# A decode-attention kernel whose second result row is gathered to one partition: two column pieces of 256 and 320, two copies, one run of 1152 bytes

## Chip, cores, metric

One core of one Trainium2 chip. The metric is the device time of one execution in microseconds (us), median over the runs named. Each kernel's time is set beside runs of the kernel before on the same chip in the same rounds. All runs count as fast or, single ones, as unknown; no slow state appeared. Ratios are the mean time of one kernel's fast runs over that of the other's of the same rounds, so they are not quite the ratios of the medians that I quote.

The names in the traces: PE is TensorE, which multiplies matrices (PEld its weight loads); DVE is VectorE, ACT ScalarE, and SP the SyncE, which issues the transfers (DMA). SBUF is the on-chip memory for data, PSUM the one that takes PE's sums; both have 128 partitions, and four groups of 32 of them are called quadrants here. A transfer has landed when the last increment of its semaphore is recorded. The granted clock is the share of TensorE's full clock that the trace records. Of a store, a "run" is a piece of adjacent bytes; elsewhere a run is one execution.

## The reference

Two problems A and B of the same shape: one token, 32 query heads, 16 key/value heads, head size 128, model width 576. A attends to the last 2048 positions of its cache, B to all 8192.

```python
q = (x @ wq).reshape(B, Sq, Hq, Dh)            # 576 -> 32 heads x 128
scores = einsum("bhqd,bhkd->bhqk", q, k) * Dh ** -0.5
o = einsum("bhqk,bhkd->bhqd", softmax(scores), v)
out = o.reshape(B, Sq, Hq * Dh) @ wo           # 4096 -> 576
# result: concat([A's out, B's out]), shape (1, 1, 1152), bf16
```

## The kernel before

Only the end matters: the last product with `wo`, the copy of the sums out of PSUM, and the store. The 4096 rows of `wo` are taken as 32 "rows" jj of 128 partitions each; each row's 576 columns are cut in pieces, and piece j accumulates in partition 32·j of one PSUM bank. Only partition 32·j of each quadrant holds a result.

```python
OUTS = [2, 4]                                  # A in 2 pieces of 288 columns, B in 4 of 144

def wo_part(P, lo, n, off, res):               # rows lo .. lo+n of problem P
    def mm(pe):
        for jj in range(lo, lo + n):
            w = DM // OUTS[P]
            for j in range(OUTS[P]):
                o = off + (jj - lo) * DM + j * w
                ins = pe.matmul(ktps[P][32 * j:32 * j + 32, 0:w], lhsT=opj[:, P, jj:jj + 32],
                                rhs=slots[:, o:o + w], start=(jj == 0), stop=(jj == HQ - 1))
        return ins
    add("pe", mm, reads=[("opj", P)] + res, writes=[("bank", P)])

def finish_out(P):
    n = OUTS[P]
    add("dve", lambda dve: dve.tensor_copy(outsb[0:32 * n, P, 0:DM // n], ktps[P][0:32 * n, 0:DM // n]),
        reads=[("bank", P)], writes=[("outsb", P)])
    # ... then SP stores n runs, one from each partition 32*j
# ...
wo_loads = [(0, 0, 32, ...),                   # A, all 32 rows in one load
            (1, 0, 21, ...), (1, 21, 7, ...), (1, 28, 3, ...), (1, 31, 1, ...)]   # B in four loads
for P, lo, n, off, res in wo_loads:
    load_wo(P, lo, n, off, res)
combine([NG - 1])                              # last group's heads, waits for DVE
o_columns(1)
for P in range(2):
    ...                                        # wo_part of each load of P, then
    finish_out(P)
```

The program orders its own instructions: `add` names what each reads and writes, and semaphore waits follow. One rule of it plays a part:

```python
for r in op.reads:
    w = self.writer.get(r)
    if w is not None:
        deps.append((w, True))
    if r[0] == "bank":                         # PSUM: a reader also waits for earlier readers
        deps += [(o, False) for o in self.readers.get(r, ())]
```

Of the kernel before, what the change touches and what calls it, by code (L numbers as in the profile page):

```python
# [4 lines left out]
BF16 = mybir.dt.bfloat16  # L5
F32 = mybir.dt.float32
ALU = mybir.AluOpType
ACT = mybir.ActivationFunctionType
# [5 lines left out]
DM = 576  # L14
# [4 lines left out]
NG = 5  # L19
NKT = 4  # L20
WQ_W = 18432
OUTS = [2, 4]


class Op:
# [11 lines left out]
class Program:  # L37
# [15 lines left out]
    def add(self, eng, fn, reads=(), writes=(), dma=None, after=(), tag=None, inc=1, loop=None):  # L53
        op = Op(eng, fn, tuple(reads), tuple(writes), dma, tag, inc if dma is None or inc > 1 else 16, loop)
        deps = []
# [4 lines that stand above are left out]
            if r[0] == "bank":  # L60
                deps += [(o, False) for o in self.readers.get(r, ())]
        for r in after:
            deps += [(o, False) for o in self.readers.get(r, ())]
        for r in op.writes:
            w = self.writer.get(r)
            if w is not None:
                deps.append((w, False))
            deps += [(o, False) for o in self.readers.get(r, ())]
        for r in op.reads:
            self.readers.setdefault(r, []).append(op)  # L70
        for r in op.writes:
            self.writer[r] = op
            self.readers[r] = []
        for o, raw in deps:
            if o is op:
                continue
            if o.dma is None and o.eng == eng and (not raw or eng in ("pe", "sp")):
                continue
            op.deps.append(o)
            o.needed = True  # L80
        op.order = len(self.ops)
        self.ops.append(op)
        return op
# [192 lines left out]
def bass_concat_heads__sliding_block_cached__gqa_block_cached__decode_kernel(  # L276
# [31 lines left out]
    add = prog.add  # L308
# [28 lines left out]
    acc = nc.alloc_sbuf_tensor("acc", [128, NG, DH], F32)  # L337
    accs = nc.alloc_sbuf_tensor("accs", [128, NG, DH], F32)
    opj = nc.alloc_sbuf_tensor("opj", [128, 2, 64], BF16)
    outsb = nc.alloc_sbuf_tensor("outsb", [128, 2, DM // 2], BF16)  # L340
    warm = nc.alloc_sbuf_tensor("warm", [128, 8], F32)

    ktps = [nc.alloc_psum_tensor("ktps%d" % b, [128, 512], F32) for b in range(4)]
# [73 lines left out]
    def load_v(g):  # L417
# [19 lines left out]
        reads=["ident"], writes=["twice"])  # L437
    add("pe", lambda pe: pe.matmul(misc[:, 320:338], lhsT=twice[:, :], rhs=xnine[:, :, :].rearrange("p a r -> p (a r)"),  # L438
                                   start=True, stop=True),
        reads=[("xnine", 0), ("xnine", 1), "twice"], writes=[B_M])  # L440
# [243 lines left out]
    def wo_part(P, lo, n, off, res):  # L684
        def mm(pe):
            for jj in range(lo, lo + n):
                w = DM // OUTS[P]
                for j in range(OUTS[P]):
                    o = off + (jj - lo) * DM + j * w
                    ins = pe.matmul(ktps[P][32 * j:32 * j + 32, 0:w], lhsT=opj[:, P, jj:jj + 32],  # L690
                                    rhs=slots[:, o:o + w], start=(jj == 0), stop=(jj == HQ - 1))
            return ins
        add("pe", mm, reads=[("opj", P)] + res, writes=[("bank", P)])


    def finish_out(P):
        n = OUTS[P]
        add("dve", lambda dve: dve.tensor_copy(outsb[0:32 * n, P, 0:DM // n], ktps[P][0:32 * n, 0:DM // n]),  # L698
            reads=[("bank", P)], writes=[("outsb", P)])

        def put(eng):
            src = bass.AP(tensor=outsb, offset=P * DM // 2, ap=[[32 * DM, n], [1, DM // n]])
            dst = out[0, 0:1, P * DM:(P + 1) * DM].rearrange("o (j n) -> (o j) n", j=n)
            return eng.dma_start(dst, src)
        add("sp", put, reads=[("outsb", P)], writes=[("out", P)], dma="out%d" % P)


    WQ = [(4 * SLOT - WQ_W, [("v", 2)]), (SLOT, [("k", 1, 0), ("k", 1, 1), ("v", 0)])]
    for P in range(2):
        off, res = WQ[P]  # L710
# [10 lines left out]
        reads=["kindA"], writes=["sameA"])  # L721
# [3 lines left out]
        reads=["sameB0"], writes=["sameB"])  # L725
# [3 lines left out]
    def pick_A(dve):  # L729
# [8 lines left out]
        reads=["sameB0", "pickB"], writes=["pickB"])  # L738
# [3 lines left out]
        reads=["four"], writes=["maskP"])  # L742
# [35 lines left out]
    for P in range(2):  # L778
        for Q, lo, n, off, res in wo_loads:
            if Q == P:  # L780
                wo_part(P, lo, n, off, res)
        finish_out(P)
    prog.emit()
    for P in range(2):
        o = prog.writer[("out", P)]
# [28 lines left out]
```

## Time and profile before

| | |
|---|---|
| time, median | 245.98 us (245.89 to 246.21, 3 runs) |
| span in the profile | 244.6 us |
| share of the load queue, 16 DMA engines | 98.1% |
| B's last weights land | 242.24 us |
| PE's last matmul ends | 242.54 us |
| store issued / last increment of its semaphore | 242.92 / 244.54 us |

Times inside a run are counted from the span's start. A line of the timeline gives start, duration, engine, source line, operation, tiles, count, and in brackets how long the engine was idle before and what ended that. Where I give a third decimal, it is from the trace's single records of instructions, DMA packets and semaphore increments. The lines themselves stand in the prediction below.

### The profile page before, as it was taken

The page shows a single profiled execution, that of the slowest core. Times are in us where ns is not written, and L with a number is a line of the kernel's source. Part 1 is how long each engine was busy: PE and PEld are TensorE (multiplying, and loading weights), DVE is VectorE, ACT ScalarE, POOL GpSimd, SP SyncE. Part 2 cuts the span into 40 slices and gives each one's busy share as a digit, 9 for nine tenths or more (in the row PEclk, how much of TensorE's full clock was granted, in tenths as well). Part 3 has the DMA queues.
Part 4 walks back from the last instruction along what each step waited for, and adds up shares of the span by engine and source line. Part 5 has one row for each costly group of instructions (what it writes and reads, how often), then busy time and mean ns, then how long its engine had stood idle before and what let it go on. Part 6 is the DMA issues. An engine that isn't in the chain of part 4 may idle for free. (4 is left out here: it accounts for less than half of the span.)

```text
span 244.6 us, 5211 instructions
## 1 busy us (share of the span) xinstructions
PE 165.4 (68%) x2325; PEld 121.3 (50%) x2325; DVE 88.2 (36%) x152; ACT 92.7 (38%) x95; POOL 6.3 (3%) x33
## 2 busy tenths in 40 slices
PE   0007339968389995393999362999457799945965
PEld 0002139746236773233887221987232787624854
DVE  0001407864316454203556302455322246543031
ACT  2000016855306686102678300687600378630000
POOL 5000100000000000000000000000000000000000
PEclk9999957997759999569899859799957589975599
DMA  9999999999999999899999999999989999989993
GB/s 338 434 410 418 434 437 426 429 426 426 445 426 430 482 407 450 380 439 429 478 439 429 413 418 429 434 504 397 461 375 434 429 488 397 461 388 428 414 409 135
DMA packets 4068, 102.88 MB, mean 421 GB/s; under 512 B 602, under 2 KB 732, under 8 KB 988
## 3 DMA queue, kind: packets, MB, share of 16 engines
q1 hardware_dynamic: 3900, 102.76, 98.1%
q8 instruction: 6, 0.10, 0.2%
q10 hardware_dynamic: 160, 0.00, 0.0%
q14 instruction: 2, 0.02, 0.0%
HBM read 102.76 MB, written 0.00 MB: 420 GB/s over the span
## 5 line engine op out<-in xcount | busy, mean ns | idle before, releaser
L506 ACT ACTIVATE kt<-ktps 128x1024 bf16<-128x1024 bf16 x80 | 79.5, 1036 | 89.6 <-PE ktps L496 89.6
L496 PE MATMUL ktps<-ident,slots 128*128 128x128 bf16 x1280 | 87.8, 234 | 22.5 <-PEq L214 19.2
L496 PEld LDWEIGHTS ktps<-ident,slots 128*128 128x128 bf16 x1280 | 81.7, 106 | 38.0 <-issue 37.9
L509 DVE COPY kt<-ktps 128x1024 bf16<-128x1024 bf16 x80 | 60.7, 768 | 59.0 <-PE ktps L496 59.0
L588 PE MATMUL opsum<-slots,ptm 128*32 128x512 bf16 x320 | 28.5, 532 | 9.8 <-PEq L214 9.8
L521 PE MATMUL sacc<-kt,qst 128*32 128x512 bf16 x320 | 25.4, 392 | 2.2 <-PEq L214 2.2
L588 PEld LDWEIGHTS opsum<-slots,ptm 128*32 128x32 bf16 x320 | 14.0, 129 | 22.9 <-issue 20.6
L559 PE MATMUL misc<-ident,psb 128*128 128x128 bf16 x40 | 4.6, 285 | 15.8 <-PEq L214 15.8
L547 ACT ACTIVATE psb<-sacc,stat 128x2048 bf16<-128x2048 f32 x5 | 9.8, 1967 | 10.1 <-DVE stat L536 10.1
L606 DVE TENSOR_TENSOR vtmp<-opsum,maskV 128x512 f32<-128x512 f32 x4 | 2.8, 692 | 30.2 <-PE opsum L588 30.2
L559 PEld LDWEIGHTS misc<-ident,psb 128*128 128x128 bf16 x40 | 3.4, 125 | 18.2 <-issue 18.2
L438 PE MATMUL misc<-xnine,twice 64*128 64x18 bf16 x1 | 0.2, 170 | 18.0 <-DMA xnine<-in_B_x_dram 18.0
L566 DVE TENSOR_TENSOR ptm<-misc,maskP 128x1024 bf16<-128x1024 bf16 x5 | 3.5, 691 | 16.0 <-PE misc L559 16.0
L521 PEld LDWEIGHTS sacc<-kt,qst 128*32 128x32 bf16 x320 | 5.0, 94 | 8.3 <-issue 4.6
L438 PEld LDWEIGHTS misc<-xnine,twice 64*128 64x128 bf16 x1 | 0.1, 99 | 18.0 <-issue 18.0
L462 ACT ACTIVATE qrow<-opsum 128x512 bf16<-128x512 f32 x1 | 0.6, 597 | 19.4 <-PE opsum L456 19.4
L690 PE MATMUL ktps<-slots,opj 128*32 128x144 bf16 (+1 forms) x192 | 6.7, 247 | 0.7 <-issue 0.5
L690 PEld LDWEIGHTS ktps<-slots,opj 128*32 128x32 bf16 x192 | 5.3, 96 | 1.9 <-issue 0.6
L447 DVE TENSOR_SCALAR xpad<-misc,par 128x5 bf16<-128x5 f32 (+1 forms) x8 | 1.2, 229 | 13.8 <-PE misc L438 13.8
L481 POOL COPY qst<-qcol 128x32 bf16<-128x32 bf16 x8 | 1.7, 211 | 147.4 <-PE sacc L521 147.4
L559 PE MATMUL turned<-ident,psb 128*128 128x128 bf16 x40 | 5.3, 313 | 0.0
L534 DVE TENSOR_REDUCE stat<-sacc 128x1 f32<-128x512 f32 x5 | 3.5, 691 | 4.4 <-PE sacc L521 4.4
(75 smaller groups left out, 52.9 us busy)
## 6 DMA issues: line engine op xcount, KB each, us to landing
slots<-in_B_k_cache_dram SPq DMA_DIRECT2D x8, 4096.0 KB
slots<-in_A_k_cache_dram SPq DMA_DIRECT2D x4, 2048.0 KB
slots<-in_A_v_cache_dram SPq DMA_DIRECT2D x4, 2048.0 KB
slots<-in_A_wq_dram SPq DMA_DIRECT2D x1, 4608.0 KB, 13.8
slots<-in_B_wq_dram SPq DMA_DIRECT2D x1, 4608.0 KB, 24.0
slots<-in_A_wo_dram SPq DMA_DIRECT2D x1, 4608.0 KB, 18.7
slots<-in_B_wo_dram SPq DMA_DIRECT2D x1, 3024.0 KB, 25.5
slots<-in_B_wo_dram SPq DMA_DIRECT2D x1, 1008.0 KB, 7.7
```

The source lines that it names most:

```text
L481: return pool.tensor_copy(dst, src)
L496: ins = pe.matmul(ktps_bf[q][:, t * 128:(t + 1) * 128], lhsT=slots[:, o:o + 128], rhs=ident[:, :], start=True, stop=True, is_transpose=True)
L506: add("act", lambda act, src=src, dst=dst: act.activation(dst, src, ACT.Copy), reads=[("bank", q)], writes=[("kt", u % NKT, q)], tag="e%d% ...
L509: add("dve", lambda dve, src=src, dst=dst: dve.tensor_copy(dst, src), reads=[("bank", q)], writes=[("kt", u % NKT, q)], tag="e%d%d" % (u, q))
L521: ins = pe.matmul(sacc[32 * j:32 * j + 32, :], lhsT=qst[:, o:o + 32], rhs=rhs, start=(u == 0 and e == 0), stop=True, skip_group_check=True)
L534: add("dve", lambda dve: dve.tensor_reduce(st(C_M + g), sacc[:, :], AX.X, ALU.max), reads=[B_S], writes=[("st", C_M + g)], tag="max")
L547: return act.activation(dst, src, ACT.Exp, bias=st(C_NB + g), scale=SCALE, accum_out=st(C_L + g))
L559: ins = pe.matmul(dst[:, t * 128:(t + 1) * 128], lhsT=psb[:, o:o + 128], rhs=ident[:, :], start=True, stop=True, is_transpose=True)
L566: return dve.tensor_tensor(ptm[:, c * 1024:(c + 1) * 1024].rearrange("p (t y) -> p t y", t=8), dst.rearrange("p (t y) -> p t y", t=8), mas ...
L588: ins = pe.matmul(opsum[64 * j + 32 * x:64 * j + 32 * x + 32, :], lhsT=ptm[:, o:o + 32], rhs=v[:, at[0], at[1], :, :, b:b + 128], start=(n ...
L606: add("dve", lambda dve: dve.tensor_tensor(vtmp[:, :, :], src, by, ALU.mult), reads=[B_O, w], writes=["vtmp"], tag="keep")
L690: ins = pe.matmul(ktps[P][32 * j:32 * j + 32, 0:w], lhsT=opj[:, P, jj:jj + 32], rhs=slots[:, o:o + w], start=(jj == 0), stop=(jj == HQ - 1))
```

## The change

The intent: a store of one run instead of four needs all of B's result in one partition. Two pieces instead of four, one for DVE and one for ACT, keep the copies at one for each engine, and the widths 256 and 320 balance the two engines. A stays as it was.

```diff
-OUTS = [2, 4]
+PIECES = [[288, 288], [256, 320]]
...
-                w = DM // OUTS[P]
-                for j in range(OUTS[P]):
-                    o = off + (jj - lo) * DM + j * w
+                for j, w in enumerate(PIECES[P]):
+                    o = off + (jj - lo) * DM + sum(PIECES[P][:j])
...
+    def finish_B():
+        lo = 0
+        for j, (name, w) in enumerate(zip(("dve", "act"), PIECES[1])):
+            def go(eng, j=j, lo=lo, w=w):
+                dst, src = outsb[0:1, DM + lo:DM + lo + w], ktps[1][32 * j:32 * j + 1, 0:w]
+                return eng.activation(dst, src, ACT.Copy) if j == 1 else eng.tensor_copy(dst, src)
+            add(name, go, reads=[("bank", 1)], writes=[("outsb", 1, j)]).key = ("out", "piece")
+            lo += w
+        add("sp", lambda sp: sp.dma_start(out[0, 0:1, DM:2 * DM], outsb[0:1, DM:2 * DM]),
+            reads=[("outsb", 1, j) for j in range(2)], writes=[("out", 1)], dma="out1")
```

## The prediction

> **What bounds the kernel now**
>
> I read the page's share of DMA and its queues first, then the chain that ended last, then the instructions of the last ten microseconds one by one.
>
> The page of the kernel before:
>
> ```profile
> q1 hardware_dynamic: 3900, 102.76, 98.1%
> HBM read 102.76 MB, written 0.00 MB: 420 GB/s over the span
> ```
>
> The SP load queue keeps the 16 DMA engines busy for 98% of the span. For some 240 us the kernel is a stream of loads, and this change touches no load. It touches only what follows the last bytes, so the question is what the tail is worth. The chain in order of time, window 233 to 246 us:
>
> ```profile
> 233.52 8.35 DMA slots<-in_B_wo_dram
> 241.87 0.04 issue
> 241.92 0.65 PE ktps L690 x16
> 242.56 0.02 issue
> 242.59 0.31 DVE outsb L698
> ```
>
> Columns: start, duration, what. The last of B's output weights land at 241.87 and 242.24; 16 matmuls, one DVE copy, and the store of the result follow. The timeline of the same tail shows how PE came there:
>
> ```profile
> 235.74 4.79 PE L690 MATMUL ktps<-slots,opj 128*32 128x288 bf16 x136
> 239.25 0.45 DVE L698 CAST outsb<-ktps 64x288 bf16<-64x288 f32 x1 [3.62 <-PE ktps L690]
> 239.73 3.77 SPq L704 DMA_DIRECT2D out_dram<-outsb  x2
> 240.98 0.68 PE L690 MATMUL ktps<-slots,opj 128*32 128x144 bf16 x30 [0.46 <-issue]
> 241.92 0.62 PE L690 MATMUL ktps<-slots,opj 128*32 128x144 bf16 x16 [0.26 <-DMA slots<-in_B_wo_dram]
> 242.59 0.31 DVE L698 CAST outsb<-ktps 128x144 bf16<-128x144 f32 x1 [2.89 <-PE ktps L690]
> ```
>
> Brackets: idle time before, and what ended it. PE does 64 matmuls of A (32 rows in 2 pieces), then 128 of B (32 rows in 4 pieces). It has slack in B: it idles 0.46 and 0.26 us waiting for weights. So the end hangs on loads now, but with PE only about 1.3 us behind (the gaps below). This is the number that decides.
>
> By groups, window 228 to 246 us (last columns: busy us, mean ns; idle):
>
> ```profile
> L690 PE MATMUL ktps<-slots,opj 128*32 128x288 bf16 x64 | 4.1, 286 | 0.0
> L690 PE MATMUL ktps<-slots,opj 128*32 128x144 bf16 x128 | 3.1, 228 | 0.7 <-issue 0.5 <-DMA slots<-in_B_wo_dram 0.3
> L698 DVE CAST outsb<-ktps 64x288 bf16<-64x288 f32 x1 | 0.5, 450 | 3.6 <-PE ktps L690 3.6
> L698 DVE CAST outsb<-ktps 128x144 bf16<-128x144 f32 x1 | 0.3, 307 | 2.9 <-PE ktps L690 2.9
> ```
>
> B has twice A's matmuls and takes less PE time: in B four matmuls stream side by side, in A two. The single records of the trace give the pitch. In A a pair starts at 235.368, 235.490, 235.613 ... 238.920: 122.5 ns per row. In B a set of four starts every 62.5 ns (239.105, 239.168, 239.230). Both are columns/2.4 ns + 2.5 ns: 288/2.4 = 120, 144/2.4 = 60. A row costs the time of its widest piece, not the sum of its pieces.
>
> **What the Trainium skill says**
>
> - "TensorE: Matmul & The Clock Gate", Part 3 (packing small matmuls): matmuls on different column tiles run concurrently and start about 4 ns apart. The trace agrees: the two of a pair start 4 ns apart (238.798, 238.802). So fewer, wider pieces use fewer of the four tiles.
> - "PSUM — Partial Sum Buffer", "PSUM bank collisions raise a hardware error": two engines may not touch one bank in the same 32-partition quadrant at once; different quadrants are allowed. The two copies read partitions 0 and 32, so hardware would let them overlap. No run here shows it yet, and this program orders them anyway (below).
> - "ScalarE: Activation LUTs", "What ACT_TABLE_LOAD costs": an ACTIVATE with immediate scale takes 186 ns + 0.833 ns per column, and copy is in every table set. The trace agrees: 512 fp32 columns out of PSUM took 597 ns (the page says 612), and only one table load stands in the whole trace although Copy and Exp alternate.
> - "Perfetto Trace Analysis", HWDGE part of the lifecycle: the record of a DMA instruction ends when its descriptors are made; data and receipt come later. Here the store was issued at 242.924, its record is 0.572 long, its 4 packets of 288 bytes ran at 244.135 to 244.217 at 20 to 22 ns each, and the four engines' increments arrived at 244.485 to 244.543: 1.62 us in all, of which bytes are almost nothing.
>
> **The change part by part**
>
> *Matmuls.* B's rows become one of 256 and one of 320 columns on two tiles: 64 matmuls instead of 128. By A's law a row costs 320/2.4 + 2.5 = 135.8 ns instead of 62.5. B's first row may start when A's last pair has streamed, 239.047 for the second tile (seen before as well). Then:
> - rows 0 to 20 end their streaming at 239.047 + 21 × 0.1358 = 241.90, where it was 240.35 before. Their followers' weights have been there since 240.935.
> - rows 21 to 27: to 242.85; their followers' weights came at 241.87.
> - rows 28 to 30: to 243.26; the last weights came at 242.24.
> So after the change PE never waits for weights in B: it becomes the bound of the tail. The last row starts at 239.047 + 31 × 0.1358 = 243.257. A matmul's record is 166 ns + columns/2.4 (226 at 144, 286 at 288), so 299 at 320: end 243.556. Before, the last one started at 242.299 and ran 238, end 242.537. **+1.02 us**, all on the path.
>
> *Copies.* Removed: a copy of 128 partitions × 144, 307 ns. Added: DVE 1 × 256 and ACT 1 × 320. Partitions go in parallel, so one partition saves nothing and the length costs: from 307 at 144 and 450 at 288, 0.993 ns per column, 256 take 418 ns. For ACT: 597 at 512 columns and 1023 median at 1024, 0.83 per column, so 320 take about 438 ns.
> They look parallel, but the program's bookkeeping says otherwise: each read of a "bank" also depends on every earlier reader of it on another engine. ACT's read of bank 1 comes second, so ACT waits for DVE's copy. The hand-over from DVE to ACT is 34 ns in this trace (DVE's stat result ends 222.097, ACT's exponent starts 222.131). So 418 + 34 + 438 = 890 instead of 307: **+0.58 us**, all on the path, since the store waits for both. PE to DVE stays 51 ns, copy to SP 29 ns, as before.
>
> *Store.* Four runs of 288 bytes on four engines become one of 1152. The loads' packets of 1152 bytes took 51 ns, against 22 now: +0.03; the stagger of four engines, 244.485 to 244.543, goes: −0.06. Issue, latency and receipt stay (A's store of two runs also took 1.62 us, 239.729 to 241.350). **−0.03 us**. If the one run is cut over 16 engines into 72-byte pieces, it may instead be +0.1. The closing barrier was over 0.35 us before the store landed and is not on the path.
>
> *Moved, without effect.* A's part is the same apart from its layout in SBUF; 64 fewer weight loads sit on a PE that was not bound by them.
>
> Sum: 1.02 + 0.58 − 0.03 = +1.57 us. The median before is 245.98, so **247.5 us**, +0.6%.
>
> **The rivals**
>
> 1. *The fewer matmuls win.* If PE were bound by the number of instructions, halving B's would shorten it. For: 64 weight loads fewer. Against: the pitch is exactly columns/2.4 + 2.5 in both A and B. PE would still end no earlier than the last weights allow: 242.29 + 0.30 = 242.59, and the time would be 245.98 + 0.05 + 0.58, some 246.6.
> 2. *The two copies overlap.* If my reading of the bookkeeping is wrong, they take 438 ns together, +0.13 instead of +0.58: about 247.1. For it speaks that hardware could; against it, the dependency rule quoted above.
> 3. *The single run is much cheaper to store.* If short writes of 288 bytes cost a read-modify-write in the receipt, some tenths might go. Against: the runs of 576 bytes of A took as long as those of 288. It could give at most the 0.33 us between packet and increment: 247.2.
> 4. *Hidden by loads.* If the unprofiled runs have the last weights later than this trace (the loads run at full rate and could vary by half a microsecond), part of PE's 1.02 is hidden: some 247.0. The profiled run took 246.14, near the median, which speaks against.
>
> None reaches 2%, which is 4.9 us; the whole tail after the last weights is 2.3 us.
>
> **Range and chances**
>
> PE's term is a law fitted on two widths in this trace (± 0.1, more if rival 4 holds), the copies ± 0.1 if ordered and −0.45 if not, the store ± 0.15, run to run ± 0.16 from the three times. Together 247.0 to 248.0 should hold it eight times in ten. Within 2%: 0.98; each side 0.01, for causes outside the tail.
>
> **What would show it right or wrong**
>
> - Matmul records of B in 128x256 and 128x320 forms, rows starting every 136 ns from about 239.0 to 243.3 without an idle gap; no wait of PE for B's output weights. Gaps there would refute the +1.02.
> - The chain of waits should run from B's first matmuls through PE, no longer through the load of the weights.
> - A DVE record of about 0.42 and an ACT record of about 0.44 that starts after it and waits for DVE. Overlapping records refute the +0.58.
> - From the store's issue to the last increment about 1.6 us; one packet of 1152 bytes.
> - Rows at 62 ns, or a last matmul ending before 243.0, would mean that I have the tiles wrong.

## The result, and the profile after

| | before | changed |
|---|---|---|
| median, 6 runs each | 245.97 us (245.87 to 246.43) | 246.45 us (246.26 to 246.98) |
| ratio | | 1.0018, 95% interval 1.0005 to 1.0031 |
| span in the profile | 244.587 | 244.969 |

The change is slower by half a microsecond, within 2%. The direction was predicted, the size (+1.57) was not, and the median lies below the range. The timeline of the changed kernel's tail:

```profile
238.06 0.59 SPq L702 DMA_DIRECT2D out_dram<-outsb  x1
238.34 4.19 PEld L689 LDWEIGHTS ktps<-slots,opj 128*32 128x32 bf16 x64 [1.11 <-DMA slots<-in_B_wo_dram]
238.34 4.52 PE L689 MATMUL ktps<-slots,opj 128*32 128x256 bf16 x64 [0.80 <-DMA slots<-in_B_wo_dram]
242.90 0.41 DVE L711 CAST outsb<-ktps 1x256 bf16<-1x256 f32 x1 [4.87 <-PE ktps L689]
243.35 0.43 ACT L711 ACTIVATE outsb<-ktps 1x320 bf16<-1x320 f32 x1 [22.38 <-DVE outsb L711]
243.80 0.28 SPq L714 DMA_DIRECT2D out_dram<-outsb  x1
```

(The label 128x256 of the PE line covers both widths.) B is now one stretch of 64 matmuls without an idle gap of PE; ACT starts when DVE has ended; and the record of B's store is 0.28 long, where A's, still of two runs, is 0.59. One thing is not as predicted at first sight: B starts after an idle gap of 0.80, ended by a load.

The single records show more than the line: the two pieces of a row do not keep in step. The 320-column matmuls follow each other every 136 ns from the first to the last. The 256-column ones start every 109 ns, run up to four rows ahead of their partners, and then wait for weights themselves: row 21 starts at 240.757 (its load landed at 240.713), row 28 at 241.817 (241.773). These two waits cost nothing, since the wide piece ends last.

The chain that ended last says the same from the end backwards (start, duration, what):

```profile
211.78 26.52 DMA slots<-in_B_wo_dram
238.30 0.04 issue
238.34 4.54 PE ktps L689 x55
242.88 0.02 issue
242.90 0.42 DVE outsb L711
243.32 0.02 issue
243.35 0.43 ACT outsb L711
```

Before, the load in this chain was the one of B's rows 28 to 30, landing at 241.87. Now it is the one of B's *first* 21 rows, landing at 238.30, and 4.5 us of PE follow it.

The two spans differ by 0.382 us, and the tail accounts for all of it:

| step of the tail (single records) | before | changed | difference | predicted |
|---|---|---|---|---|
| PE's last matmul ends | 242.537 | 242.864 | +0.327 | +1.02 |
| from there to the store's issue | 0.387 | 0.936 | +0.549 | +0.58 |
| issue to last increment of the store | 1.619 | 1.124 | −0.495 | −0.03 |
| sum | | | +0.381 | +1.57 |

So two terms need explaining: why PE lost 0.33 and not 1.02, and where the store's half microsecond comes from. Theory T is this sum of three terms; its rivals are named with each experiment.

### The profile page after: what moved, and what is told of

The parts are those of the page before. It is cut to its first block, busy times and chain, and to the rows that moved or that the text cites. A ratio compares the mean times of both kernels' runs of the same rounds, so it can differ in the third digit from the quotient of the medians.

```text
span 245.0 us, 5084 instructions
## 1 busy us (share of the span) xinstructions
PE 164.6 (67%) x2261; PEld 119.1 (49%) x2261; DVE 88.1 (36%) x152; ACT 92.9 (38%) x96; POOL 6.3 (3%) x33
## 5 line engine op out<-in xcount | busy, mean ns | idle before, releaser
L496 PE MATMUL ktps<-ident,slots 128*128 128x128 bf16 x1280 | 85.3, 230 | 18.7 <-PEq L214 17.4
L496 PEld LDWEIGHTS ktps<-ident,slots 128*128 128x128 bf16 x1280 | 79.3, 104 | 34.2 <-issue 34.1
L588 PE MATMUL opsum<-slots,ptm 128*32 128x512 bf16 x320 | 29.2, 543 | 14.2 <-PEq L214 14.2
L689 PE MATMUL ktps<-slots,opj 128*32 128x288 bf16 (+2 forms) x128 | 8.6, 287 | 0.8 <-DMA slots<-in_B_wo_dram 0.8
L689 PEld LDWEIGHTS ktps<-slots,opj 128*32 128x32 bf16 x128 | 6.7, 97 | 2.3 <-DMA slots<-in_B_wo_dram 1.1
```

The costliest lines, as they stand in the source:

```text
L496: ins = pe.matmul(ktps_bf[q][:, t * 128:(t + 1) * 128], lhsT=slots[:, o:o + 128], rhs=ident[:, :], start=True, stop=True, is_transpose=True)
L588: ins = pe.matmul(opsum[64 * j + 32 * x:64 * j + 32 * x + 32, :], lhsT=ptm[:, o:o + 32], rhs=v[:, at[0], at[1], :, :, b:b + 128], start=(n ...
```

## The experiments

### The changed kernel again (r_after)

No edit.

> The changed kernel again, on the same chip as the next three. Theory T: the change is a sum of three terms on the tail: PE later by 0.3 to 1.0 us (B's rows at 135.8 ns; 0.3 if A's matmuls end before B's first weights land, 1.0 if A's matmuls end last because the clock was halved during the last group), the ordered copies +0.56, the store -0.49. Expected +0.4 to +0.6 against before, and in the profile a store of about 1.1 us from issue to last increment against 1.6. Rival (only the store's receipt got cheaper): the time between the packet and the increment should be shorter than the 0.33 us of before.

Measured: 246.49 (246.35 to 247.17, 5 runs) against 245.99; ratio 1.0028 (1.0015 to 1.0041). The store took 1.134 us. The rival about the receipt fails: from the start of the data packet to the last increment it is 0.375 us here, against 0.35 before (first packet 244.135, last increment 244.485 to 244.543). What got shorter lies ahead of the packet: issue to first packet 1.211 before, 0.759 here.

### Copies not ordered (par)

```diff
-        add("pe", mm, reads=[("opj", P)] + res, writes=[("bank", P)])
+        add("pe", mm, reads=[("opj", P)] + res, writes=[("bank", P), ("sum", P)])
...
-            add(name, go, reads=[("bank", 1)], writes=[("outsb", 1, j)]).key = ("out", "piece")
+            add(name, go, reads=[("sum", 1)], writes=[("outsb", 1, j)]).key = ("out", "piece")
```

> The changed kernel with ACT's copy no longer ordered behind DVE's (they read different quadrants of the bank). Theory T: copies take the longer of 0.41 and 0.43 plus 0.03, not 0.90: 0.42 us less than the changed kernel, so about equal to before (245.9 to 246.1). Rival (two engines reading one bank hold each other up, or the store waits for something else): no gain, 246.4 to 246.5.

Measured: 246.01 against 245.99 for before and 246.49 for the changed kernel on the same chip; ratio to before 1.0009 (0.9996 to 1.0022). Timeline of its tail:

```profile
242.99 0.43 ACT L711 ACTIVATE outsb<-ktps 1x320 bf16<-1x320 f32 x1 [21.79 <-PE ktps L689]
242.99 0.41 DVE L711 CAST outsb<-ktps 1x256 bf16<-1x256 f32 x1 [4.35 <-PE ktps L689]
243.44 0.28 SPq L714 DMA_DIRECT2D out_dram<-outsb  x1
```

Both copies start on PE's last matmul and take what they took alone; the result was correct, as the Trainium skill ("PSUM — Partial Sum Buffer", "PSUM bank collisions raise a hardware error") lets one expect of different quadrants. The store's issue moves from 0.937 after PE's end (r_after) to 0.490. The order that the program's own rule makes is thus worth 0.45 us, and with it goes nearly all of the change's loss.

### Before, with B in two pieces (width2)

```diff
-OUTS = [2, 4]
+OUTS = [2, 2]
```

> The kernel before with B in two pieces of 288 instead of four of 144; one DVE copy of 64x288, store of two runs. Theory T: rows at 122.5 ns; PE ends only 0 to 0.05 us later than before if B's first weights set its start (238.34 + 31 x 0.1225 + 0.286 = 242.43, less than the last weights allow), up to 0.6 later if A ends late; the copy 450 instead of 307 ns; the store unchanged at 1.6 us. Together +0.15 to +0.3 against before. The prediction as written (start always at A's end) says +0.6 and +0.14 = +0.74. If fewer matmuls help, it is faster than before.

Measured: 246.12 against 245.99; ratio 1.0014 (1.0001 to 1.0027), that is +0.13 by the medians and +0.34 by the means, where +0.15 to +0.3 was expected. PE's last matmul ends at 242.43 in a run where B's first weights landed at 238.24; the copy takes 0.45 and the store 1.545. Halving the number of matmuls wins nothing: PE does end 0.11 earlier than in the trace of before, but this run's last weights also landed 0.16 earlier (242.08 against 242.24). And the "start at A's end" of the prediction (+0.74) is not what the usual run does.

### A's matmuls issued earlier (early, early2, early_p1 to early_p4)

```diff
+    wo_part(*wo_loads[0])
     combine([NG - 1])
     o_columns(1)
     for P in range(2):
         for Q, lo, n, off, res in wo_loads:
-            if Q == P:
+            if Q == P and P:
                 wo_part(P, lo, n, off, res)
```

> The changed kernel with A's 64 output matmuls issued before the last combine instead of after it, so that they run while PE would idle for DVE. Theory T: A always ends before B's first weights land, PE's B rows run from that landing to 4.55 us later in every run: the median 0 to 0.3 us below the changed kernel, and no run as slow as 246.98. Rival (PE's start in B has nothing to do with A): same as the changed kernel, same spread.

Measured: 246.50 (246.28 to 248.07, 6 runs). The median is that of the changed kernel, and the spread got wider instead of narrower: the expectation missed. A ran from 231.8 on and was out of the way, yet two runs took 248.07 and 248.06. (Of all 14 runs of this kernel, the nine outside this slow group took 246.28 to 246.73, none over 246.8 as four of 13 of the changed kernel did. That is in keeping with theory T, but few runs, and sorted afterwards.) I ran it again:

> The kernel with A's matmuls issued earlier, once more, because two of its six runs took 248.07 and no other kernel did. Reading: PE now idles 2.5 us between A's end and B's first weights, and in some runs the clock is halved there; B's rows at half clock would take 270 ns until it recovers. If so some runs are again near 248, and if the profiled one is among them it shows a granted clock of 0.5 after 236 us and rows of 270 ns. If no run is slow, the two stay unexplained.

246.63 (246.29 to 247.88, 4 runs), again one slow run and not the profiled one. Two single profiles more:

> One more profile of the kernel with A's matmuls issued earlier. 246.3 to 246.6 with the clock at 1.0 from 230 us on. If it takes about 248, the reading (clock halved after 2.5 us of idle PE) expects granted clock 0.5 after 236 us and rows of about 270 ns for some microseconds; the rival (loads late) expects B's last weights over 1 us later than 242.2.

> The same as the run before it: 246.3 to 246.6 at full clock, about 248 with the clock halved in the tail.

246.53 and 246.37, the clock at 1.0 throughout the tail. And the last two:

> As the two profiles before: 246.3 to 246.6 at full clock; about 248 with granted clock 0.5 after 236 us and rows of about 270 ns if the reading holds.

> The same again: 246.3 to 246.6 at full clock from 230 us on; about 248 with the clock halved in the tail and B's rows 270 ns apart for some microseconds.

248.10 and 248.14: both caught it. The next lines show PE by stretches of time (columns: stretch, its length, PE busy us and count, granted clock, DMA share, GB/s). First early_p3:

```profile
236.00:238.40 2.40, 0.00 (x0) 1.00 0.91 379
238.40:241.80 3.40, 3.34 (x29) 0.50 0.63 253
```

Then early, whose profiled run was not slow, in the same stretches:

```profile
236.00:238.40 2.40, 0.00 (x0) 1.00 0.93 387
238.40:241.80 3.40, 3.38 (x53) 1.00 0.63 249
```

Same loads, same start of B, but 29 recorded matmuls instead of 53 in the same 3.4 us: at the granted clock of 0.5 B's 320-column matmuls are 267 ns apart (238.701, 238.968, 239.235), at 1.0 they are 136. B's last weights landed at 242.26, so late loads are not it. PE had idled 3.08 us before B. The Trainium skill ("TensorE: Matmul & The Clock Gate", Part 1: The HAM clock gate) says that after an idle window of about 3.4 us the clock falls to half, and that the windows run free of the kernel. 5 of 14 runs of this kernel took 247.88 or more, and the halved stretch lasted 3.4 us in both traces (238.4 to 241.8, 239.2 to 242.6).

The traces allow a closer look at what decides. In all 20 traces each stretch of one granted clock, but for the last one that the trace's end cuts off, is a whole multiple of 3.413 us, so the windows' edges can be carried on into the tail:

| trace | PE idle before B | most of it in one window of 3.41 us | clock halved after it |
|---|---|---|---|
| early_p2 | 1.63 | 0.89 | no |
| early_p1 | 1.66 | 0.87 | no |
| early | 2.54 | 1.42 | no |
| early2 | 2.80 | 1.69 | no |
| early_p4 | 3.00 | 2.66 | yes |
| early_p3 | 3.08 | 3.01 | yes |

The idleness within one window fits, and so does the plain length of the gap: the two halved traces have the longest gaps as well. No run separates the two. What the table does show is that a window need not be idle throughout: in early_p4 B's matmuls were running for its last 0.76 us.

### PE loaded with 14 more rows ahead of A (pad_before, pad_after)

```diff
+    def pad(pe):
+        for r in range(14):
+            for j in range(2):
+                ins = pe.matmul(ktps[2][32 * j:32 * j + 32, 0:288], lhsT=opj[:, 0, r:r + 32],
+                                rhs=slots[:, r * DM + j * 288:r * DM + j * 288 + 288], start=True, stop=True)
+        return ins
+    add("pe", pad, reads=[("opj", 0)] + wo_loads[0][4], writes=[("bank", 2)])
```

> The kernel before with 28 more matmuls of 288 columns (14 rows, 1.7 us at 122.5 ns, into a bank nobody reads) ahead of A's output matmuls: A ends 1.7 us later. Theory T: PE has that slack in the kernel before, since its rows of B take 62.5 ns and it waits for the last weights: 0 to +0.1 us.

> The changed kernel with the same 28 matmuls. Theory T: now B starts at A's end instead of at its first weights, and every row of B counts: PE's end is A's end plus 4.35, so +0.7 to +1.3 us against the changed kernel, 247.1 to 247.8: the branch that the prediction took for the usual one. Rival (PE's end is not what the tail waits for): 246.5, as without the extra matmuls.

Measured: pad_before 246.15 against 246.05, ratio 0.9999 (0.9983 to 1.0014); pad_after 248.04 (246.75 to 248.59) against 246.05, ratio 1.0062 (1.0034 to 1.0091). The same 1.7 us of PE work costs the kernel before nothing and the changed one about 1.5 us (248.04 against 246.49; different chips, so only roughly). That is above my range of +0.7 to +1.3: in the profiled run A would have ended late even without the extra rows, which I had not added in. Timeline, pad_before and then pad_after:

```profile
241.78 0.86 PE L690 MATMUL ktps<-slots,opj 128*32 128x144 bf16 x44
242.69 0.31 DVE L698 CAST outsb<-ktps 128x144 bf16<-128x144 f32 x1 [1.57 <-PE ktps L690]
```

```profile
241.72 3.29 PE L689 MATMUL ktps<-slots,opj 128*32 128x320 bf16 x43
245.05 0.41 DVE L711 CAST outsb<-ktps 1x256 bf16<-1x256 f32 x1 [3.89 <-PE ktps L689]
```

A ends at 240.63 and 240.67 in the two. With 62.5 ns a row, B still catches up with its last weights (PE's end 242.645, theirs to land 242.12); with 136 ns it ends at 245.01.

### The changed kernel's own late runs (after_p1, after_p2)

No edit; what was asked for was a profile of one of its runs above 246.8.

> One more profile of the changed kernel. If it takes 246.3 to 246.6, A ends before B's first weights land (238.3 to 238.5). If it takes over 246.8, theory T expects A's last matmul after 238.5, B's first row right behind it, rows at 136 ns; the rival (rows slower than 136 ns, or last weights late) shows another spacing or a late landing.

> The same as the run before it: 246.3 to 246.6 with A early, over 246.8 with A late.

Measured 247.24 and 246.68. The first caught the late branch. The chain of waits of after_p1:

```profile
234.04 1.03 DVE accs L391
235.07 0.04 issue
235.11 0.34 PE ktps L671 x5
...
235.55 8.17 PE ktps L689 x111
243.72 0.02 issue
243.75 0.42 DVE outsb L711
```

No load is in it after 234 us: A and B's output matmuls are one piece of 8.17 us. Set in order of A's end, five traces show how it comes about ("halved until" is the end of the last stretch of granted clock 0.5 before the tail):

| trace | halved until | A's last matmul ends | B's first weights land | PE's last matmul ends |
|---|---|---|---|---|
| changed | 229.6 | 237.54 | 238.30 | 242.864 |
| r_after | 230.0 | 238.15 | 238.39 | 242.960 |
| after_p2 | 230.9 | 238.78 | 238.61 | 243.180 |
| before | 231.2 | 239.21 | 238.40 | 242.537 |
| after_p1 | 231.3 | 239.36 | 238.50 | 243.709 |

In the changed kernel PE ends 4.5 to 4.6 us after the later of two things: the landing of B's first weights, or A's end less 0.16 (A's last pair overlaps B's first). The loads hardly move between runs, 238.3 to 238.6. A's end moves by 1.8 us, in step with the end of the halved stretch that lies over the last group's work on PE (an agreement of five traces; no run changed the clock alone). The kernel before does not care, since it waits for its last weights anyway: its runs span 245.87 to 246.43, those of the changed kernel 246.26 to 247.24.

### Two equal pieces, unordered, one run (best)

```diff
-PIECES = [[288, 288], [256, 320]]
+PIECES = [[288, 288], [288, 288]]
```
with the edit of par.

> The changed kernel with unordered copies and B in two pieces of 288 columns each: rows at 122.5 ns so that PE is again limited by the last weights, both copies side by side (DVE 450, ACT about 405 ns), the one-run store. Theory T: against before PE 0 to -0.05, copies +0.14, store -0.49: 245.65 to 245.75, 0.3 us faster. Rival (the store was cheap in the changed kernel only because it was issued later, after all loads had drained): the store takes 1.5 again, no gain against before.

Measured: 245.72 (245.55 to 245.86, 5 runs) against 246.07; ratio 0.9983 (0.9970 to 0.9997). Timeline:

```profile
242.74 0.40 ACT L711 ACTIVATE outsb<-ktps 1x288 bf16<-1x288 f32 x1 [21.57 <-PE ktps L689]
242.74 0.45 DVE L711 CAST outsb<-ktps 1x288 bf16<-1x288 f32 x1 [4.65 <-PE ktps L689]
243.22 0.28 SPq L714 DMA_DIRECT2D out_dram<-outsb  x1
```

PE ended at 242.70, 4.20 after B's first weights landed (238.50), with rows 122.5 ns apart and one pause of 0.05 at row 28, whose weights landed at 241.99. The last row followed row 30 without a pause, although its weights (242.355) had come only 0.06 before it started. PE and the loads are about level here, and the expectation that the last weights would limit PE missed. The store took 1.136 although it was issued 0.58 us earlier than in the changed kernel (243.217 against 243.800): the rival that it was cheap there for being late fails. This version beats the kernel before by a third of a microsecond, and the changed one by about 0.7 (245.72 against 246.45 and 246.49, other chips).

### The store in two, four and sixteen runs (gap2, gap4, gap16)

The kernel best, but blocks of the result kept apart in the same partition, so that they can't be joined to one run. Core of the edit for four runs (two and sixteen: blocks of 288 and 36 columns, 320 and 40 apart):

```diff
+                dst = bass.AP(tensor=outsb, offset=DM + 320 * j, ap=[[DM + 640, 1], [160, 2], [1, 144]])
+                src = ktps[1][32 * j:32 * j + 1, 0:w].rearrange("p (r c) -> p r c", r=2)
...
+            src = bass.AP(tensor=outsb, offset=DM, ap=[[DM + 640, 1], [160, 4], [1, 144]])
+            return sp.dma_start(out[0, 0:1, DM:2 * DM].rearrange("o (j n) -> o j n", j=4), src)
```

> The kernel of two pieces of 288 with unordered copies, but the two halves kept 64 bytes apart in the one partition, so that the store has two runs of 576 bytes (two engines). Theory S1 (what the one run saves is the making of the descriptors of a store on several engines, ahead of the first packet): record of the store back at 0.5 to 0.6, first packet 1.2 us after the issue instead of 0.75, 0.4 us slower than one run. Theory S2 (runs under 512 bytes cost more at the receipt): 576 is above, no change. Theory S3 (reading several partitions costs): one partition, no change.

> The same with four blocks of 144 columns kept apart in the one partition: four runs of 288 bytes, as before, from one partition instead of four. S1: 1.5 to 1.6 us from issue to last increment, 0.4 to 0.45 slower than one run. S2: slower than one run too, but in the time after the packet (over 0.4 instead of 0.33 to 0.38), and slower than two runs of 576. S3: 1.13 us, as one run.

> The same with sixteen blocks of 36 columns kept apart: sixteen runs of 72 bytes, one for each of 16 engines. If what costs in S1 is the number of engines, it is the slowest (1.7 or more). If it is the increments that the issuing sequencer has to add for engines not used (12 or 14 of 16 with four or two engines, none with 16), the record is short again, 0.3 to 0.45 as those of the weight loads on 16 engines (0.33 to 0.44). S2: slowest at the receipt.

The issue of each store on SP, from the timelines of gap2, gap4 and gap16:

```profile
243.16 0.63 SPq L717 DMA_DIRECT2D out_dram<-outsb  x1
```
```profile
242.91 0.67 SPq L717 DMA_DIRECT2D out_dram<-outsb  x1
```
```profile
242.94 0.62 SPq L717 DMA_DIRECT2D out_dram<-outsb  x1
```

| runs x bytes, partitions | median us | issue record | issue to first packet | issue to last increment |
|---|---|---|---|---|
| 1 x 1152, one (best) | 245.72 | 0.277 | 0.753 | 1.136 |
| 2 x 576, one (gap2) | 246.24 | 0.630 | 1.279 | 1.655 |
| 4 x 288, one (gap4) | 246.28 | 0.673 | 1.320 | 1.729 |
| 16 x 72, one (gap16) | 246.16 | 0.616 | 1.266 | 1.765 |
| 4 x 288, four (before) | 246.07 | 0.572 | 1.211 | 1.619 |

S1 holds in the main: as soon as there is more than one run, 0.51 to 0.57 us is added ahead of the first packet, somewhat more than the 0.4 to 0.45 expected (in width2, two runs from two partitions, the first packet comes 1.156 after the issue, 0.40 more than in best). S2 fails: runs of 288 and 72 bytes take no longer than one of 1152 from their last packet to the last increment (0.356 in gap4, 0.368 in gap16, 0.383 in best). S3 fails: reading one partition alone saves nothing. The two finer readings of S1 fail too: the cost is a step from one to several, not a slope in their number, and sixteen runs have the long record as well. (In the traces the store of one run has two updates of its semaphore, the first 0.31 ahead of the packet; the stores of two and four runs have three and five, the first again 0.2 ahead of all packets; the store of sixteen has sixteen, all after the first packet. So with one run the early update is there and the record short, with sixteen it is missing and the record long: it is not what costs. Which engine moved a packet is not in the traces.) Whether the step comes with the second run or with the second engine stays open: every way I found to cut 1152 bytes changes both.

### Four pieces with a one-run store (four1)

```diff
+PIECES = [[288, 288], [144] * 4]
...
+        for j, (name, w) in enumerate(zip(("dve", "act") * 2, PIECES[1])):
```
with the edit of par, ACT taking pieces 1 and 3.

> The kernel before with the one-run store as the only gain: B stays in four pieces of 144 (rows at 62.5 ns), each copied to the one partition, two by DVE and two by ACT, unordered, then one store of 1152 bytes. Theory T: PE unchanged, store -0.49, copies a little longer than before's one (two short copies in a row on each engine, some 0.5 to 0.55 instead of 0.31, worked out from DVE's 307 ns and the 0.2 us spacing of its small operations in this trace): +0.2 to +0.25. Together -0.25: 245.75 to 245.85, and a spread like before's. Rival (the gain of the two-piece kernel is from elsewhere): equal to before or slower.

Measured: 245.78 (245.70 to 246.27, 5 runs) against 246.11; ratio 0.9993 (0.9979 to 1.0007). In the trace the store takes 1.126, PE ends at 242.515, and from there to the issue it is 0.708 against 0.387 before: +0.32, where +0.2 to +0.25 was expected, since the second copy of an engine starts 0.31 to 0.33 after the first. The medians differ by −0.33, the two profiled spans by −0.19 (store −0.49, copies +0.32, PE −0.02), and the interval reaches past 1, so by runs alone the gain is not secured. In the trace the one-run store keeps its gain with PE's slack kept.

## Why the prediction was wrong

By the profiled spans the sum missed by 1.19 us (+1.57 against +0.38): 0.69 of it is PE's start, 0.47 the store, 0.03 the copies.

- **PE, +1.02.** The law was right for the piece that ends last: the 320-column matmuls came 136 ns apart (135.8 predicted) without a wait. The 256-column ones did not share that pitch (109 ns) and waited twice for weights, against the sign "no wait of PE for B's output weights", but off the path. (The 240.935 given for the landing of rows 21 to 27 belongs to another load; theirs landed at 240.814, which changes no sum.) The failed step is "B's first row may start when A's last pair has streamed, 239.047". That start was read from one trace, in which A happened to end after B's first weights (239.21 against 238.40). In the kernel before this is harmless and so can't be seen in its times. In the usual run of the changed kernel A ends earlier, and B starts when the weights land, 238.3 to 238.4: PE's end is then +0.33 to +0.42. The predicted branch exists: after_p1, 247.24, with PE's end +1.17. But it is the rarer one: of 13 runs of the changed kernel three took over 246.9.
- **Copies, +0.58.** Right: +0.549, ordered as the bookkeeping said, DVE 0.411 (0.418 predicted), ACT 0.428 (0.438), and par showed that the order alone is 0.45 of it.
- **Store, −0.03.** Mis-sized: −0.495. The prediction priced bytes, stagger and receipt, and took "issue, latency and receipt stay" as given because two runs took as long as four. Both are on the same side of the step between one run and several. Its rival 3 expected at most 0.33 and looked for it after the packet; it lies ahead of the packet.
- **The rivals.** Fewer matmuls (1) did not win. Overlapping copies (2) were not what happened, but par shows that they can (both start at 242.988). Hidden by loads (4) came nearest to PE's miss, with the sign of the cause turned: not later last weights, but an earlier A.
- **The range.** 247.0 to 248.0 treated PE's term as ± 0.1 because it was fitted on durations; the start it was added to was the uncertain number. With the store right, the same branch would have given 245.98 + 1.02 + 0.58 − 0.50 = 247.1, and the usual one gives 246.4.

## What to carry to other kernels

When work that had slack becomes the bound, its start matters as much as its speed: look for what else could release it, and take more than one trace, because slack hides the variation of what runs ahead. Read a program's own dependency rules before counting two engines as parallel; here they turned 0.43 us into 0.87. A small final store to HBM was half a microsecond shorter as a single run, which is worth gathering for if the gathering costs less than that and the engines that gather run side by side.

## What the Trainium skill lacked or had wrong

- "DMA: Bandwidth & Descriptors" (Latency and other measured facts) gives about 0.6 us to the first byte for a DMA issued by SP, without a dependence on the number of runs or engines. Here the first packet started 0.75 us after the issue with one run, and 1.16 (width2) to 1.32 with 2, 4 or 16. The step, some 0.4 to 0.6 us, is not on the page.
- The same page (Specifications) says that transfers under 512 bytes are read, changed and written back. No cost of that showed in these stores: from the last packet to the last increment 0.356 us with 288 bytes and 0.368 with 72, against 0.383 with 1152.
- "ScalarE: Activation LUTs" ("What ACT_TABLE_LOAD costs") gives 186 ns + 0.833 ns a column for a tile of 128 partitions, an estimate of 453 ns for 320 columns; measured 428, with one partition.
- "TensorE: Matmul & The Clock Gate" has two figures for the idle gaps of PE to avoid: over about 3.4 us ("HAM oscillation") and over about 3 us (the table of "Why this matters for your kernels"). Here gaps of 3.00 and 3.08 us (early_p4, early_p3) were followed by 3.4 us at half clock, which cost 1.6 us, and gaps of up to 2.80 were not. The first figure is too long for these traces; the second fits them.
